# Fused block-causal attention and top-2 expert layer: noise through one dense load, constants set later, a finer router schedule

## The chip, the cores and the metric

One core of a Trainium2 chip runs the kernel. The metric is the device time of one execution in microseconds (us). Of the kernel before, four executions were timed.

## The reference

Eight batches of eight heads, 576 tokens, head size 64. Attention is causal in blocks of 64 tokens. Its output, 4608 rows of 512, goes through a noisy top-2 router with eight experts and then through the two chosen experts.

```
scores = where(block_i >= block_j, q @ k.T / 8, -1e9)
x      = softmax(scores) @ v                    # (8,8,576,64) -> (4608, 512)
noisy  = x @ w_gate + log1p(exp(x @ w_noise)) * noise        # (4608, 8)
two largest per row, softmax over the two -> weights
out    = sum over the two experts e: weight * (relu(x @ w1[e]) @ w2[e])
```

w1 is 8 x 512 x 1024, w2 is 8 x 1024 x 512.

## The kernel before, in words

**Attention.** The work is cut into four groups of two batches (g = 0 to 3; NG = 4). A group has 26 score units (UG = 26): two sets of four head pairs, with 12 units of 512 columns and one small closing unit per set (UN = 13). `score_unit` (line 270) does the matmuls of q and k into one of two PSUM buffers and one exponential on ScalarE (line 287). `av_tile` (line 307) multiplies the exponentials with v, nine tiles (TG = 9) per set, and DVE (VectorE) divides by the sums (lines 335 and 336) into `xr`. `transpose_qk` (line 226) turns the loaded q and k of a group into `qT` and `kT` with matmuls against an identity into one of two buffers of `tr_ps`, which DVE copies out (lines 251 and 253). A group's q and k come in five chunks, 4, 0, 1, 2, 3; of chunk 4 the halves "4A" and "4B" are transposed apart.

**Router.** `x_transpose` (line 343) transposes a group's output, `router` (line 356) is a generator: each `yield` ends a step, and `router_step` runs one step. Its parts are the logits (line 361), noise (371), the largest and second largest (375 to 385), counting within a row (391 to 401), counting matmuls over rows (`pp`, lines 405 and 406), places in the experts' lists (409 to 435) and a record for each row (438 to 450). `scatter` (line 464) then writes each row twice into the experts' lists in DRAM (`xd`) by an indirect DMA of the POOL queue. Groups 0 and 1 form half 0 of the lists, groups 2 and 3 half 1.

**Experts.** Sixteen blocks in the order SEQ (line 593), one expert and half each, 640 rows. `layer1` (line 534) has eight steps with ReLU on ScalarE (line 544), `layer2` (line 548) five. A row's first expert leaves its result in `yd` (line 559, SP queue); the second gathers it (`gather`, line 575, POOL queue), adds (line 562) and writes the output rows (line 564, POOL queue). `load_x` (line 483) fetches a block's rows with a transposing DMA on the SP queue.

**Order.** The order is written out by hand. `at(slot, fn, ...)` (line 600) puts a call into a slot; slot u is what follows score unit u, 104 units in all, then one slot per layer step. Lines 662 to 720 hold the slots: `s0` is a group's first slot, `r0 = s0 + 26`; `rsl` lists the slot of each router step, `r1` the slot of the first scatter. Each engine and each DMA queue executes its own instructions in this order; a scatter or gather also waits for the last ScalarE instruction but one (`pace`), and the loads made with `after` wait for a score unit. `raw_pool` holds eight chunks each of q and k.

**Start.** Lines 644 to 660: the identity, the loads of chunks 4, 0 and 1 on POOL, the constants (`setup_consts`, line 138, on DVE and POOL), chunks 2 and 3, v, the gate weights, and the transposes of 4B and 0. The noise comes in 72 small DMAs of the SP queue, 18 a group (`nz_job`, line 618), 64 rows of 32 bytes each. `clear_x` (line 610) zeroes the part of each list that may stay unwritten, 16 DMAs of 96 rows for each half.

Of the kernel before, what the change touches and what calls it, by code (L numbers as in the profile page):

```python
# [19 lines left out]
def kernel(  # L20
# [110 lines left out]

    nz_all = keep.tile([P, NT, E], F32)
    slots = keep.tile([P, NT, 2], I32)
    wts = keep.tile([P, 2, NT], F32)
    oh_all = keep.tile([P, NG, 2, E, TG], BF16)
    zero = keep.tile([P, 528], BF16)

    def setup_consts():
        nc.vector.memset(ones_mat, 1.0)
        nc.vector.memset(rmask, 1.0)  # L140
        nc.vector.memset(rmask[:, :, :, 0:1], 0.0)
        nc.vector.memset(emask, 1.0)
        nc.vector.memset(emask[:, :, 0:1], 0.0)
        for e in range(E):
            nc.gpsimd.memset(lims[:, e:e + 1], float(e * CAP + LT[e] * P))
        nc.vector.memset(zero, 0.0)
# [11 lines left out]
        nc.gpsimd.iota(poff[:, 0:1], pattern=[[0, 1]], base=0, channel_multiplier=1)  # L158
        nc.vector.tensor_scalar(poff[:, 1:2], poff[:, 0:1], 7, 3, op0=ALU.bitwise_and,
                                op1=ALU.logical_shift_left)  # L160
# [7 lines left out]
        nc.gpsimd.iota(rowid_i, pattern=[[CAP, E], [P, CT]], base=0, channel_multiplier=1)  # L168
# [42 lines left out]
    def load_w(pool, e, k=None):  # L211

        if not k:
            wload[e] = (pool.tile([P, DB, F], BF16, tag="w1", name="w1sb"),
                        pool.tile([P, FB, Dm], BF16, tag="w2", name="w2sb"))
        for t, src in zip(wload[e], (moe_w1[e], moe_w2[e])):
            n = t.shape[1]
            w = src.rearrange("(b p) c -> p b c", p=P)
            if k is None:
                nc.gpsimd.dma_start(out=t, in_=w)  # L220
            elif (k < 2) == (n == DB):
                b0 = (k % 2) * n // 2
# [133 lines left out]
    def router(g):  # L356
# [31 lines left out]
        nc.vector.tensor_add(m.rearrange("p t e -> p e t"), oh[:, 0], oh[:, 1])  # L388

        c2 = rt.tile([P, TG, E], F32, tag="c2")  # L390
        nc.vector.tensor_tensor_scan(out=c2.rearrange("p t e -> p (t e)"),
# [6 lines left out]
        nc.vector.tensor_tensor(out=msv[0], in0=msv[1], in1=m, op=ALU.subtract)  # L398

        w2 = rt.tile([P, TG], F32, tag="w2")  # L400
        nc.vector.tensor_sub(w2, mx[:, 0, :, 0], mx[:, 1, :, 0])
        yield
# [3 lines left out]
        nc.tensor.matmul(out=pp[:, 1, :], lhsT=prem, rhs=mf, start=True, stop=True)  # L406
        nc.scalar.activation(out=w2, in_=w2, func=AF.Exp)
        incl = rt.tile([P, 2, E, TG], F32, tag="incl")
        nc.vector.tensor_tensor_scan(out=incl.rearrange("p i e t -> p (i e t)"),
# [42 lines left out]

    RSTEPS = 12
    rgen = {}
# [28 lines left out]
    def load_x(b):  # L483
        half, e = SEQ[b]
        xg = (ffn["x"] if b else xa_pool).tile([P, DB, CAP], BF16, tag="xg", name="xg")
        ins = nc.sync.dma_start_transpose(out=xg, in_=xd[half][e * CAP:(e + 1) * CAP, 0:Dm])
# [88 lines left out]
    def gather(b, c):  # L575

        half, e = SEQ[b]
        yg = ffn["y"].tile([P, Dm], BF16, tag="yg", bufs=GB, name="yg")
        if len(gathers) < GB:
            nc.gpsimd.memset(yg, 0.0)  # L580
        gathers.append(b)
# [28 lines left out]
    def clear_x(half, slot):  # L610

        for e in range(E):
            r0 = max(0, min(82 * e - 48, CAP - 192)) + e * CAP
            for r in (r0, r0 + 96):
                ins = nc.sync.dma_start(out=xd[half][r:r + 96, :], in_=zero[0:96, 0:DR])
                after(ins, slot)

    def nz_job(g, slot):
        for idx in range(TG):
            for p0, tok in token_blocks(g, idx):  # L620
                ins = nc.sync.dma_start(out=nz_all[p0:p0 + 64, g * TG + idx, :],
                                        in_=token_order(moe_noise[tok:tok + 64, :]))
                after(ins, slot)

# [17 lines left out]
    sched.__enter__()  # L642

    make_identity(nc, ident_f)
    nc.vector.tensor_copy(ident, ident_f)
    load_qk(0, (4, 0, 1))
    for i in range(2):
        nc.vector.memset(vt[i][:, :, :, D:D + 1], 1.0)
    setup_consts()
    load_qk(0, (2, 3))  # L650
    load_v(0)
    nc.gpsimd.dma_start(out=wgn[:, :, 0:E], in_=moe_w_gate.rearrange("(b p) e -> p b e", p=P))
# [9 lines left out]
    for g in range(NG):  # L662
        s0 = g * UG
        if g + 1 < NG:
            at(s0 + 13, transpose_qk, g + 1, "q", "4B")
            at(s0 + 13, transpose_qk, g + 1, "k", "4B")
            at(s0 + 14, transpose_qk, g + 1, "q", 0)
            at(s0 + 15, transpose_qk, g + 1, "k", 0)
            at(s0 + 18, transpose_qk, g + 1, "q", 1)
            at(s0 + 20, transpose_qk, g + 1, "k", 1)  # L670
            at(s0 + 18, load_qk, g + 1, (2, 3))
            at(s0 + 11, load_v, g + 1)
        if g + 2 < NG:
            at(s0 + 20, load_qk, g + 2, (4, 0, 1))
        at(s0 + 0 + (g == 0), transpose_qk, g, "q", 2)
        at(s0 + 1 + (g == 0), transpose_qk, g, "k", 2)
        at(s0 + 11, transpose_qk, g, "q", 3)
        at(s0 + 12, transpose_qk, g, "k", 3)
        at(s0 + 16, transpose_qk, g, "q", "4A")
        at(s0 + 17, transpose_qk, g, "k", "4A")  # L680
        at(s0 + 6, nz_job, g, s0 + 5)
        for i in range(TG):
            at(s0 + UN + 2 + i, av_tile, g, 0, i)
        r0 = s0 + UG
        if g + 1 < NG:
            for i in range(TG):
                at(r0 + 2 + i, av_tile, g, 1, i)
            for j in range(5):
                at(r0 + min(5 + 2 * j, 12), x_transpose, g, j)
            rsl = [13, 14, 15, 16, 17, 18, 19, 20, 20, 21, 21, 22]  # L690
            r1 = 23
        else:
            for i in range(TG):
                at(r0 + i // 2, av_tile, g, 1, i)
            for j in range(5):
                at(r0 + 2 + j, x_transpose, g, j)
            rsl = [7, 8, 8, 9, 9, 10, 11, 12, 12, 13, 13, 14]
# [38 lines left out]
    for fn, b, j in steps:  # L736
# [115 lines left out]
```

## Time and profile before

| what | value |
|---|---|
| median of four executions | 560.83 us (557.41 to 564.97) |
| the profiled execution's own time | 564.97 us |
| its span, first to last instruction | 563.0 us |
| instructions | 9912 |
| TensorE matmuls busy | 445.5 us (79%) |
| ScalarE busy | 238.8 us (42%) |
| POOL busy | 261.5 us (46%) |
| DVE busy | 175.0 us (31%) |
| mean granted TensorE clock | 0.862 |

The profile is of one execution. Its busy rows cut the span into 40 slices of 14.1 us; each digit is a busy share in tenths. A timeline row gives the start, the time taken, the engine, the line, the operation and tiles, the count, and in brackets the idle time of the engine before it with what ended that idle time. PE is TensorE, PEld its weight loads, ACT ScalarE, DVE VectorE, POOL GpSimd, SPq the DMA queue of SyncE. A group row gives busy time, the mean time of one instruction and idle time.

### The profile page before, as it was taken

The page shows a single profiled execution, that of the slowest core. Times are in us where ns is not written, and L with a number is a line of the kernel's source. Part 1 is how long each engine was busy: PE and PEld are TensorE (multiplying, and loading weights), DVE is VectorE, ACT ScalarE, POOL GpSimd, SP SyncE. Part 2 cuts the span into 40 slices and gives each one's busy share as a digit, 9 for nine tenths or more (in the row PEclk, how much of TensorE's full clock was granted, in tenths as well). Part 3 has the DMA queues.
Part 4 walks back from the last instruction along what each step waited for, and adds up shares of the span by engine and source line. Part 5 has one row for each costly group of instructions (what it writes and reads, how often), then busy time and mean ns, then how long its engine had stood idle before and what let it go on. Part 6 is the DMA issues. An engine that isn't in the chain of part 4 may idle for free.

```text
span 563.0 us, 9912 instructions
## 1 busy us (share of the span) xinstructions
PE 445.5 (79%) x3928; PEld 267.4 (47%) x3944; DVE 175.0 (31%) x490; ACT 238.8 (42%) x319; POOL 261.5 (46%) x311
## 2 busy tenths in 40 slices
PE   3787966796649688995939999997957897886975
PEld 2454643463336465652515556653524454443542
DVE  4374894388327737100003000011010120202102
ACT  1756754454426414533414445553414343342330
POOL 9673454583680256675413023273250533517243
PEclk9777985687577779999869999998987997978899
DMA  9999997296289967887776767999999726524122
GB/s 140 142 158 232 96 211 175 81 105 96 91 170 176 164 141 158 202 210 160 150 104 136 162 132 125 187 197 166 129 104 195 188 83 113 156 55 156 43 94 85
DMA packets 141205, 79.76 MB, mean 142 GB/s; under 512 B 101621, under 2 KB 131063, under 8 KB 141152
## 3 DMA queue, kind: packets, MB, share of 16 engines
q0 software_dynamic: 70560, 55.79, 62.7%
q1 hardware_dynamic: 70592, 23.27, 23.2%
q8 instruction: 33, 0.54, 0.4%
q14 instruction: 20, 0.16, 0.1%
HBM read 68.28 MB, written 34.21 MB: 182 GB/s over the span
## 4 chain that ended last, share of the span: by engine, by line
issue 31%; PE 27%; POOL 15%; DMA 11%; DVE 11%; ACT 2%; POOLq 1%; another core or an unknown queue 1%; DVEq 0%; SPq 0%; ACTq 0%
PE yp L553 8%; PE hp L541 7%; POOL yg L582 5%; DMA yg<-yd,orow 4%; POOL out_dram L564 4%; POOL xd L467 4%; PE sc L284 3%; PE av L321 3%; PE tp L246 3%; DMA xg<-xd 2%; DMA w1sb<-in_moe_w_dram 2%; DVE hq L253 2%; DMA t<-in_k_dram 2%; PE av L332 2%; DVE xr L336 2%
## 5 line engine op out<-in xcount | busy, mean ns | idle before, releaser
L541 PE MATMUL hp<-xg,w1sb 128*128 128x320 bf16 x1024 | 159.6, 316 | 40.1 <-ACT hq L544 31.5
L553 PE MATMUL yp<-w2sb,hq 128*128 128x512 bf16 x624 | 144.7, 387 | 9.3 <-DVE yo L562 8.3
L541 PEld LDWEIGHTS <-w1sb 128*128 128x128 bf16 x1024 | 104.6, 103 | 92.5 <-issue 36.2
L544 ACT ACTIVATE hq<-hp 128x640 bf16<-128x640 f32 x128 | 89.4, 704 | 114.8 <-PE hp L541 84.4
L287 ACT ACTIVATE esc<-sc 128x1024 bf16<-128x1024 f32 x96 | 94.8, 1027 | 86.4 <-PE sc L284 49.8
L562 DVE SCALAR_TENSOR_TENSOR yo<-yp,wrow,yg 128x512 f32<-128x512 f32 x46 | 34.5, 751 | 291.3 <-ACT ysb L558 186.0
L467 POOL DMA_INDIRECT xd<-xr,slots x72 | 71.7, 996 | 74.0 <-issue 48.7
L564 POOL DMA_INDIRECT out_dram<-yo,trow x46 | 46.7, 1015 | 125.6 <-DVE yo L562 109.3
L553 PEld LDWEIGHTS <-hq 128*128 128x128 bf16 x640 | 63.5, 99 | 86.1 <-issue 18.2
L558 ACT ACTIVATE ysb<-yp,wrow 128x512 bf16<-128x512 f32 x70 | 48.1, 688 | 98.2 <-PE yp L553 76.6
L582 POOL DMA_INDIRECT yg<-yd,orow x46 | 47.4, 1031 | 57.0 <-ACT hq L544 23.1
L284 PE MATMUL sc<-hq 64*128 64x512 bf16 (+4 forms) x320 | 47.5, 363 | 16.1 <-ACT esc L287 13.1
L321 PE MATMUL av<-vt,esc 128*128 128x65 bf16 x640 | 38.9, 219 | 15.5 <-DVE xr L336 6.6
L321 PEld LDWEIGHTS <-esc 128*128 128x128 bf16 x640 | 30.0, 113 | 31.8 <-issue 14.3
L206 POOL DMA_DIRECT2D vt<-in_v_dram x40 | 33.8, 875 | 14.3 <-PE av L332 10.4
L246 PE MATMUL tp<-ident,t 128*64 128x128 bf16 x512 | 28.9, 282 | 7.4 <-DVE hq L251 3.9
L336 DVE TENSOR_TENSOR xr<-av,rden 128x256 bf16<-128x256 f32 x72 | 30.6, 425 | 2.5
L246 PEld LDWEIGHTS <-t 128*64 128x64 bf16 x512 | 23.1, 148 | 15.6 <-issue 8.1
L253 DVE COPY hq<-tp 128x1024 bf16<-128x1024 bf16 (+1 forms) x24 | 25.0, 1042 | 7.9 <-PE tp L246 3.8
L284 PEld LDWEIGHTS <-hq 64*128 64x128 bf16 x320 | 12.5, 100 | 26.6 <-issue 19.2
L335 DVE RECIPROCAL rden<-av 128x4 f32<-128x4 f32 x72 | 12.5, 174 | 38.9 <-remote 9.8
L251 DVE COPY hq<-tp 128x1024 bf16<-128x1024 bf16 (+1 forms) x24 | 14.9, 620 | 23.2 <-PE tp L246 15.2
(118 smaller groups left out, 225.4 us busy)
## 6 DMA issues: line engine op xcount, KB each, us to landing
yd<-ysb SPq DMA_DIRECT2D x70, 128.0 KB
w1sb<-in_moe_w_dram POOLq DMA_DIRECT2D x16, 512.0 KB
w2sb<-in_moe_w_dram POOLq DMA_DIRECT2D x16, 512.0 KB
t<-in_q_dram POOLq DMA_DIRECT2D x16, 256.0 KB
t<-in_k_dram POOLq DMA_DIRECT2D x16, 256.0 KB
vt<-in_v_dram POOLq DMA_DIRECT2D x32, 128.0 KB
xd<-zero SPq DMA_DIRECT2D x32, 99.0 KB
nz_all<-in_moe_noise_dram SPq DMA_DIRECT2D x72, 2.0 KB
```

The source lines that it names most:

```text
L246: nc.tensor.transpose(to[64 * hf:64 * hf + 64, :, r, :], raw[:, hf, r * 64:(r + 1) * 64], ident)
L284: nc.tensor.matmul(out=sc[:, hf, off:off + z - a], lhsT=kT[sl, c0 + jt * P:c0 + jt * P + P], rhs=qT[sl, c0 + a:c0 + z], start=True, stop=True)
L287: ins = nc.scalar.activation(out=esc[:, hh, :, piece * 512:(piece + 1) * 512], in_=sc, func=AF.Exp, scale=scale)
L321: nc.tensor.matmul(out=av[:, hh, :], lhsT=esc[:, hh, hf, c:c + P], rhs=vb[:, 4 * hf + jt, h, :], start=(jt == 0), stop=(jt == ib))
L336: nc.vector.tensor_tensor(out=xr[:, idx, st * SET * D:(st + 1) * SET * D].rearrange("p (h d) -> p h d", h=SET), in0=av[:, :, 0:D], in1=rde ...
L467: ins = nc.gpsimd.indirect_dma_start(out=xd[half].bitcast(I32), out_offset=bass.IndirectOffsetOnAxis(ap=slots[:, g * TG + idx, i:i + 1], a ...
L541: nc.tensor.matmul(out=hp[:, n, 0:NW], lhsT=w1sb[:, db, fb * P:(fb + 1) * P], rhs=xgs[b][:, db, n * NW:(n + 1) * NW], start=(db == 0), sto ...
L544: ins = nc.scalar.activation(out=hs[b][:, fb, :].rearrange("p (n w) -> p n w", n=2), in_=hp[:, :, 0:NW], func=AF.Relu)
L553: nc.tensor.matmul(out=yp, lhsT=hs[b][:, fb, c * P:(c + 1) * P], rhs=w2sb[:, fb, :], start=(fb == 0), stop=(fb == FB - 1))
L558: nc.scalar.activation(out=ysb, in_=yp, func=AF.Copy, scale=w)
L564: ins = nc.gpsimd.indirect_dma_start(out=out, out_offset=bass.IndirectOffsetOnAxis(ap=trow[half][:, e, c:c + 1], axis=0), in_=yo, in_offse ...
L582: ins = nc.gpsimd.indirect_dma_start(out=yg, out_offset=None, in_=yd[half][0:e * CAP, :], in_offset=bass.IndirectOffsetOnAxis(ap=orows[hal ...
```

## The change

Seven edits. The noise comes in one DMA of 72 partitions by 2 KB, into the tile that later receives the first expert block; DVE sorts it (16 copies), PE transposes it in fp32 (8 transposes), DVE copies it into place (36 copies), in slots 7 to 11 of group 0. The constants of DVE move from ahead of the first transposes to slot 6; those of POOL behind the loads of chunks 2 and 3. Chunk 4 is requested ahead of the identity. The transposes of q and k get other slots. The router has 15 steps instead of 12, with other slots; group 2's AV tiles, router and scatters run closer together. The clears have 8 DMAs of 128 rows for each half and later slots. The weights of the third and fourth expert come in two DMAs each instead of four, and the buffers of `gather` are zeroed by DVE at slot 110 instead of by POOL one at a time.

```
+    xa = xa_pool.tile([P, DB, CAP], BF16)
+    nzw = [xa.rearrange("p a b -> p (a b)")[0:B * TG, 1024 * i:1024 * (i + 1)].bitcast(F32) for i in range(2)]
...
-    def setup_consts():
-        nc.vector.memset(ones_mat, 1.0)
...
+    def setup_pool():
         for e in range(E):
             nc.gpsimd.memset(lims[:, e:e + 1], float(e * CAP + LT[e] * P))
...
         nc.vector.tensor_add(m.rearrange("p t e -> p e t"), oh[:, 0], oh[:, 1])

+        w2 = rt.tile([P, TG], F32, tag="w2")
+        nc.vector.tensor_sub(w2, mx[:, 0, :, 0], mx[:, 1, :, 0])
+        yield
+
         c2 = rt.tile([P, TG, E], F32, tag="c2")
...
-        w2 = rt.tile([P, TG], F32, tag="w2")
-        nc.vector.tensor_sub(w2, mx[:, 0, :, 0], mx[:, 1, :, 0])
+        yield
         yield
...
         nc.scalar.activation(out=w2, in_=w2, func=AF.Exp)
+        yield
         incl = rt.tile([P, 2, E, TG], F32, tag="incl")
...
-    RSTEPS = 12
+    RSTEPS = 15
...
-        yg = ffn["y"].tile([P, Dm], BF16, tag="yg", bufs=GB, name="yg")
-        if len(gathers) < GB:
-            nc.gpsimd.memset(yg, 0.0)
+        yg = ffn["yg"][len(gathers) % GB]
...
-            r0 = max(0, min(82 * e - 48, CAP - 192)) + e * CAP
-            for r in (r0, r0 + 96):
-                ins = nc.sync.dma_start(out=xd[half][r:r + 96, :], in_=zero[0:96, 0:DR])
-                after(ins, slot)
...
+            r0 = max(0, min(82 * e - 26, CAP - P)) + e * CAP
+            ins = nc.sync.dma_start(out=xd[half][r0:r0 + P, :], in_=zero[:, 0:DR])
+            after(ins, slot)
+
+    def load_nz():
+
+        nc.sync.dma_start(out=nzw[0], in_=moe_noise.rearrange("(p t) e -> p (t e)", t=64))
+
+    def sort_nz(eh):
+        e0 = eh * (E // 2)
+        src = nzw[0].rearrange("p (j r e) -> p e r j", j=8, r=8)[:, e0:e0 + E // 2]
+        dst = nzw[1].rearrange("p (e h r j) -> p h e r j", e=E // 2, h=2, r=8)
+        for hf in range(2):
+            for e in range(E // 2):
+                nc.vector.tensor_copy(dst[:, hf, e], src[:, e])
+
+    def transpose_nz(eh):
+        nb = B * TG
+        e0 = eh * (E // 2)
+        tp = tr_ps.tile([P, E // 2, nb], F32, tag="tr")
+        for e in range(E // 2):
+            nc.tensor.transpose(tp[:, e, :], nzw[1][:, e * P:(e + 1) * P], ident_f[0:nb, 0:nb])
+        for hf in range(2):
+            p = slice(64 * hf, 64 * hf + 64)
+            src = tp[p].rearrange("p e (g b k) -> p e g b k", b=2, k=TG)
+            dst = nz_all[p, :, e0:e0 + E // 2].rearrange("p (g i) e -> p e g i", i=TG)
+            for bb in range(2):
+                for e in range(E // 2):
+                    nc.vector.tensor_copy(dst[:, e, :, 4 * bb:4 * bb + 4], src[:, e, :, bb, hf:8:2])
+            nc.vector.tensor_copy(dst[:, :, :, 8], src[:, :, :, hf, 8])
...
+    load_qk(0, (4,))
     make_identity(nc, ident_f)
     nc.vector.tensor_copy(ident, ident_f)
-    load_qk(0, (4, 0, 1))
+    load_qk(0, (0, 1))
+    load_nz()
...
-    setup_consts()
     load_qk(0, (2, 3))
+    setup_pool()
     load_v(0)
...
-            at(s0 + 13, transpose_qk, g + 1, "q", "4B")
-            at(s0 + 13, transpose_qk, g + 1, "k", "4B")
-            at(s0 + 14, transpose_qk, g + 1, "q", 0)
+            early = 5 if g else 0
+            at(s0 + 13 - early, transpose_qk, g + 1, "q", "4B")
+            at(s0 + 13 - early, transpose_qk, g + 1, "k", "4B")
+            at(s0 + 13, transpose_qk, g + 1, "q", 0)
             at(s0 + 15, transpose_qk, g + 1, "k", 0)
-            at(s0 + 18, transpose_qk, g + 1, "q", 1)
-            at(s0 + 20, transpose_qk, g + 1, "k", 1)
+            at(s0 + 24, transpose_qk, g + 1, "q", 1)
+            at(s0 + 25, transpose_qk, g + 1, "k", 1)
...
-        at(s0 + 0 + (g == 0), transpose_qk, g, "q", 2)
-        at(s0 + 1 + (g == 0), transpose_qk, g, "k", 2)
-        at(s0 + 11, transpose_qk, g, "q", 3)
+        at(s0 + 3, transpose_qk, g, "q", 2)
+        at(s0 + 5, transpose_qk, g, "k", 2)
+        at(s0 + 10, transpose_qk, g, "q", 3)
         at(s0 + 12, transpose_qk, g, "k", 3)
-        at(s0 + 16, transpose_qk, g, "q", "4A")
-        at(s0 + 17, transpose_qk, g, "k", "4A")
-        at(s0 + 6, nz_job, g, s0 + 5)
+        at(s0 + 17, transpose_qk, g, "q", "4A")
+        at(s0 + 18, transpose_qk, g, "k", "4A")
...
-        if g + 1 < NG:
+        if g < 2:
             for i in range(TG):
-                at(r0 + 2 + i, av_tile, g, 1, i)
+                at(r0 + 1 + i, av_tile, g, 1, i)
             for j in range(5):
-                at(r0 + min(5 + 2 * j, 12), x_transpose, g, j)
-            rsl = [13, 14, 15, 16, 17, 18, 19, 20, 20, 21, 21, 22]
-            r1 = 23
+                at(r0 + min(4 + 2 * j, 11), x_transpose, g, j)
+            rsl = [12, 13, 14, 15, 16, 17, 18, 19, 20, 21, 21, 22, 22, 23, 23]
+            r1 = 24
+        elif g == 2:
+            for i in range(TG):
+                at(r0 + 1 + 2 * i // 3, av_tile, g, 1, i)
+            for j in range(5):
+                at(r0 + (3, 5, 6, 7, 8)[j], x_transpose, g, j)
+            rsl = [9, 9, 10, 11, 12, 13, 14, 14, 15, 16, 16, 17, 17, 18, 18]
+            r1 = 19
         else:
...
-            rsl = [7, 8, 8, 9, 9, 10, 11, 12, 12, 13, 13, 14]
-            r1 = 15
+            rsl = [7, 7, 8, 9, 9, 10, 11, 11, 12, 13, 13, 14, 14, 15, 15]
+            r1 = 16
...
-            at(r0 + r1 + (j if g in (0, 2) else 2 * j // 3), scatter, g, j)
+            at(r0 + r1 + (2 * j // 3 if g else j), scatter, g, j)
...
-    at(8, clear_x, 0, 7)
-    at(UG + 8, clear_x, 1, UG + 7)
+    at(6, setup_consts)
+    at(7, sort_nz, 0)
+    at(8, transpose_nz, 0)
+    at(9, sort_nz, 1)
+    at(11, transpose_nz, 1)
+    at(UG + 4, clear_x, 0, UG + 3)
+    at(3 * UG + 4, clear_x, 1, 3 * UG + 3)
...
-        if u == 3 * UG + 18:
+        if u == 3 * UG + 19:
...
-            for k in range(4):
-                at(u + (10, 13, 16, 19)[k], load_w, wM, 2, k)
+            at(u + 10, load_w, wM, 2, "a")
+            at(u + 16, load_w, wM, 2, "b")
...
-            for k in range(4):
-                at(slot + 3 * k + 12, load_w, wL, 3, k)
+            ffn["yg"] = [ffn["y"].tile([P, Dm], BF16, name=f"yg{i}", bufs=1) for i in range(GB)]
+            for t in ffn["yg"]:
+                nc.vector.memset(t, 0.0)
+            at(slot + 14, load_w, wL, 3, "a")
+            at(slot + 20, load_w, wL, 3, "b")
```

More of the change, by code (lines that the diff above doesn't have):

```diff
@@ L136 @@
     zero = keep.tile([P, 528], BF16)
-    def setup_consts():
-        nc.vector.memset(ones_mat, 1.0)
[L140 to L143, printed above, removed]
+    def setup_pool():
         for e in range(E):
             nc.gpsimd.memset(lims[:, e:e + 1], float(e * CAP + LT[e] * P))
-        nc.vector.memset(zero, 0.0)
         nc.gpsimd.memset(prem, 0.0)
@@ L158, in setup_consts @@
         nc.gpsimd.iota(poff[:, 0:1], pattern=[[0, 1]], base=0, channel_multiplier=1)
+        nc.gpsimd.iota(rowid_i, pattern=[[CAP, E], [P, CT]], base=0, channel_multiplier=1)
+    def setup_consts():
+        nc.vector.memset(ones_mat, 1.0)
+        nc.vector.memset(rmask, 1.0)
+        nc.vector.memset(rmask[:, :, :, 0:1], 0.0)
+        nc.vector.memset(emask, 1.0)
+        nc.vector.memset(emask[:, :, 0:1], 0.0)
+        nc.vector.memset(zero, 0.0)
         nc.vector.tensor_scalar(poff[:, 1:2], poff[:, 0:1], 7, 3, op0=ALU.bitwise_and,
@@ L167, in setup_consts @@
                                 op=ALU.subtract)
-        nc.gpsimd.iota(rowid_i, pattern=[[CAP, E], [P, CT]], base=0, channel_multiplier=1)
         for i in range(NH):
@@ L211, in load_w @@
     def load_w(pool, e, k=None):
-        if not k:
+        if k in (None, 0, "a"):
             wload[e] = (pool.tile([P, DB, F], BF16, tag="w1", name="w1sb"),
                         pool.tile([P, FB, Dm], BF16, tag="w2", name="w2sb"))
-        for t, src in zip(wload[e], (moe_w1[e], moe_w2[e])):
+        for i, (t, src) in enumerate(zip(wload[e], (moe_w1[e], moe_w2[e]))):
             n = t.shape[1]
             w = src.rearrange("(b p) c -> p b c", p=P)
-            if k is None:
+            if k is None or k == "ab"[i]:
                 nc.gpsimd.dma_start(out=t, in_=w)
-            elif (k < 2) == (n == DB):
+            elif k in (2 * i, 2 * i + 1):
                 b0 = (k % 2) * n // 2
@@ L484, in load_x @@
         half, e = SEQ[b]
-        xg = (ffn["x"] if b else xa_pool).tile([P, DB, CAP], BF16, tag="xg", name="xg")
+        xg = ffn["x"].tile([P, DB, CAP], BF16, tag="xg", name="xg") if b else xa
         ins = nc.sync.dma_start_transpose(out=xg, in_=xd[half][e * CAP:(e + 1) * CAP, 0:Dm])
@@ L612, in clear_x @@
         for e in range(E):
-            r0 = max(0, min(82 * e - 48, CAP - 192)) + e * CAP
-            for r in (r0, r0 + 96):
-                ins = nc.sync.dma_start(out=xd[half][r:r + 96, :], in_=zero[0:96, 0:DR])
-                after(ins, slot)
[L618 to L623, printed above, removed]
+            r0 = max(0, min(82 * e - 26, CAP - P)) + e * CAP
[24 more added lines that the diff above has]
+            nc.vector.tensor_copy(dst[:, :, :, 8], src[:, :, :, hf, 8])
     def flags():
```

## The prediction

> **What bounds the kernel now.** I read the page's busy rows by slice first, then the list of waits, then the timeline around each gap of TensorE, then the stretch table for the granted clock.
>
> ```profile
> PE   3787966796649688995939999997957897886975
> DVE  4374894388327737100003000011010120202102
> PEclk9777985687577779999869999998987997978899
> ```
>
> TensorE (PE) is the fullest row, and its clock is the other half of the story: up to slice 15 (about 210 us, the attention and router part) it runs between half and full clock; after that (the expert part) mostly at full. So the attention part is not at a limit of work. It has 104 score units whose exponentials cost ScalarE 1.03 us each (line 287), 107 us, and takes 182 us (first scores at 12.87, last exponential at 195.3). Everything the change touches, but for one item, lies in this part. TensorE's instructions are executed in order, so one matmul that waits holds up the next scores, and with them ScalarE.
>
> The gaps that count, from the timeline (start, length, engine, line, operation, and in brackets the idle time before it and what ended it); the last line closes a gap in the expert part:
>
> ```profile
> 12.87 0.61 PE L284 MATMUL sc<-hq 64*128 64x512 bf16 x2 [1.41 <-DVE hq L253]
> 27.20 0.69 DVE L251 COPY hq<-tp 128x1024 bf16<-128x1024 bf16 x1 [7.54 <-PE tp L246]
> 49.91 1.06 PE L246 MATMUL tp<-ident,t 128*64 128x128 bf16 x16 [2.35 <-DMA t<-in_q_dram]
> 78.85 0.24 PE L405 MATMUL pp<-ms,ones_mat 128*128 128x144 bf16 x1 [2.83 <-DVE w L401]
> 79.92 0.30 PE L321 MATMUL av<-vt,esc 128*128 128x65 bf16 x4 [0.77 <-DVE xr L336]
> 86.86 2.15 PE L332 MATMUL av<-vt,esc 128*64 128x65 bf16 x40 [1.72 <-DVE xr L336]
> 130.69 0.24 PE L405 MATMUL pp<-ms,ones_mat 128*128 128x144 bf16 x1 [2.20 <-DVE w L401]
> 184.92 0.24 PE L405 MATMUL pp<-ms,ones_mat 128*128 128x144 bf16 x1 [2.22 <-DVE rden L335]
> 267.50 7.30 PE L553 MATMUL yp<-w2sb,hq 128*128 128x512 bf16 x24 [4.95 <-DVE yo L562]
> ```
>
> To be seen: in groups 0, 1 and 2 the router's counting matmul (line 405) stops TensorE for 2.2 to 2.8 us while VectorE (DVE) makes its input. In the first, lines 385 to 401 ran from 76.46 to 78.81, one router step against one slot of scores.
>
> The stretch table (length, busy time and count of PE, PEld, DVE, ACT, POOL, then clock) for the 3.3 us that begin about 1.5 us after each of the three stalls, and for the start of group 2:
>
> ```profile
> 80.40:83.70 3.30, 3.30 (x44) 2.21 (x42) 3.09 (x11) 1.97 (x2) 0.77 (x2) 0.50 1.20 237
> 87.20:107.60 20.40, 16.31 (x188) 10.02 (x188) 8.67 (x24) 10.08 (x11) 11.27 (x12) 0.50 0.48 118
> 131.60:134.90 3.30, 3.14 (x40) 1.98 (x41) 3.09 (x11) 1.09 (x2) 0.00 (x0) 0.50 1.17 176
> 186.20:189.50 3.30, 3.30 (x42) 2.17 (x41) 3.02 (x12) 2.83 (x3) 0.00 (x0) 0.50 1.40 74
> ```
>
> Each stall is followed by a stretch at half clock in which TensorE is the limit (busy 3.1 to 3.3 of 3.3).
>
> **The change part by part.**
>
> *Start and noise.* Score unit 0 waits for chunk 0 of k. Its last packet ends at 8.25, but the transposes stand until 9.55: both transpose buffers hold chunk 4B, whose copies sit on DVE behind the constants (DVE waits 4.31 us for an iota, ends them at 9.04, copies at 9.07). With the constants moved behind score unit 6, transposes of k can follow its landing. POOL issues chunk 4 about 0.7 earlier and chunks 0 and 1 some 0.4 earlier; the noise load, 147 KB on SP ahead of everything, gives back up to 0.8 (estimate at the 140 GB/s of slice 0). Chain: k landed 8.5, 16 transposes 1.06, copies 1.23 and 0.22: scores at 11.0 instead of 12.87, 1.9 gained. The identity is now made after two POOL issues (0.73 and 0.60), ready near 2.5, still ahead of chunk 4.
>
> What was in front moves into slots 6 to 11, over the 7.54 us hole shown above. Constants: about 2.6 us of DVE (from the pace at which they ran before). Noise: 16 sorting copies of 64 elements and 36 of 16 elements out of PSUM, 52 in all, which the trace does not have. Nearest row: the small independent copies of the router's record (lines 446 to 449) start 0.08 apart, giving 52 × 0.08 = 4.2. [...] Lower bound zero, if the hole takes all; upper bound 25, at the 0.48 of the small strided rows (lines 378, 388). From slot 6 (21.8) to slot 13 (28.4) there are 6.6 us. [...] What is late next: the two transpose buffers, hence the PE transposes of slots 11 to 13 and the scores behind them. Part of this is covered: at slot 15 TensorE waited 0.92 for group 1's k chunk 0 (32.67). [...] That the noise is loaded otherwise earns nothing itself: all waits for it sum to 0.2 us.
>
> *Clears and SP.* Half as many clears (16 each 96 rows become 8 of 128), each set later. SP loses 72 noise issues; the last 18 (155.8 to 167.3) stood just ahead of the transposed load at 167.98, but that load also needs scatters that POOL issued until 166.1, and its data are used near 198: nothing gained. What counts is that the clears (35.3 to 46.7) and noise packets leave the DMA engines just as group 1's chunk 2 comes in.
>
> *Moved q/k transposes.* Group 1's chunk 2 stalled TensorE for 2.35 us at 49.91. It is now transposed three to four slots later and its load has less company: gone. The stretch from 49.6 to 56.5 ran at half clock; full clock does transposes in 0.64 instead of 1.06, scores in 0.39 instead of 0.61, so about 38% of busy time goes: at 6 busy, 2.3, and I count half. **Gain 3.5.** Chunk 1 at slots 24 and 25 comes when DVE has the router behind it: zero. POOL gets a wait: k chunk 2 of the next group takes the raw buffer of chunk 4, whose last transpose is now in the same slot 18. Behind it are the loads of slot 20 and scatters; one slot, about 1.5 us, with eleven slots before the data are needed: nothing.
>
> *Router in 15 steps.* In groups 0 and 1 the counting inputs are made at slot 18 and used at slot 20. For group 2 it is one slot apart, with 1.26 us of DVE (lines 391, 397, 398) in it: at most 0.5 left over. 2.83 + 2.20 + 2.22 + 2 × 0.77 (the AV matmul behind, second stall like the one at 79.92) − 0.5 = **gain 8.3**. The wait for line 336 at 86.86 (1.72, 1.71 and 1.31 in the three groups) stays: lines 428 to 449 still share slots with the last AV tiles.
>
> *The clock after them.* [...] Other gaps are near and may pull the clock down anyhow: **gain 1.9**.
>
> *Group 2 re-timed.* The same matmuls in fewer slots of group 3, which has no next group to transpose: zero in sum. Its scatters begin four slots sooner, but POOL had drained them by 226 before, when group 3's followed at 228.09 off the router: nothing.
>
> *Expert part.* POOL is behind from 228 to 262:
>
> ```profile
> 259.16 0.57 POOL L580 MEMSET yg<- 128x512 bf16 x1
> 260.00 1.07 POOL L582 DMA_INDIRECT yg<-yd,orow  x1 [0.28 <-POOL yg L580]
> ```
>
> The gather at 260.00 is what TensorE awaits at 267.50. Ahead of it go one memset with its gap (0.84) and two of four weight issues (0.8 each): 2.5 sooner. In return ten memsets of about 0.27 (line 301's row) stand on DVE at slot 110, ahead of the last x copy that the router's matmul needs: 2.7, of which DVE's idle covers 1.0. **Gain 0.8.**
>
> *Sum.* −1.0 + 3.5 + 8.3 + 1.9 + 0.8 = 13.5. Its execution took 564.97 (span 563.0), the slowest of four; their median is 560.83. From the one 551.5, from the other 547.3; the terms are partly that execution's own bad luck, so I set **549**.
>
> **Rivals.** *The stalls move* (25 in 100): DVE has the same router work, so what leaves line 405 is waited for at line 332. Then chunk 2 gives 2.4, the router 4, clock and expert part nothing, noise costs 3.3: 560.8 − 3 = 558, range 553 to 566. For it: DVE is busy 3.0 of 3.3 in the rows above. Against: PE gaps there came from order, not sum (DVE 32.2 of 44.1 us in group 1).
>
> *The noise copies cost more than the hole holds* (15 in 100; slower). Place: group 0, slots 6 to 13. The net loss is 52c − 3.8 for a pace c. The other terms sum to 14.5, so it decides at c = 0.35, and is over 1% slower from 0.46. At the 0.48 of lines 378 and 388: 21.2 lost, 560.8 − 14.5 + 21.2 = 567.5, range 566 to 575. For it: strided operands, each a separate instruction. Against: no waits between them are needed, and their output is fp32.
>
> *The long half-clock stretches go too* (12 in 100): 87 to 108 and 138 to 155 follow router waits; 38% of 16.3 and 11.6 busy is 10.6 more: 538, range 532 to 542.
>
> **How the numbers follow.** My case has 48 in 100, with its own range 542 to 554. Faster by over 1% (under 555.2; about what a measurement can tell): 48 + 12 + 2 of the first rival = 62. Within 1%: 22, the rest of that rival less 1. Slower: 16. The range 538 to 566 leaves out some 6 below and 13 above.
>
> **What would show it.** Right: line 405 idle under 1 us in all; first scores near 11.0; no DMA wait for group 1's chunk 2; clock above 0.84 in group 1 and 0.70 in groups 2 and 3. Wrong: copies of the noise over 0.3 us apart, with ScalarE idle between 20 and 32; line 332's waits grown to 3 us; a 2 us hole before line 361 in the expert part.

## The result and the profile after

The changed kernel takes 554.12 us (median of 12 runs, 543.16 to 562.85), the kernel before 560.4 (17 runs, 555.83 to 567.1). The ratio is 0.975, 95% interval 0.970 to 0.981. It is taken over the executions within 1.5% of each kernel's fastest (4 of 12 after, 14 of 17 before; neither profiled execution is among them), and over all executions the means, 553.6 and 560.8, differ by only 1.3%. The forecast, 549 with a range of 538 to 566, holds. Its terms hold less well than its total: one had the wrong sign, and most of the others were far off in size.

The profiled execution after takes 555.2 us (span 553.4), against 564.97 (span 563.0). The rows that answer to those of before:

```profile
PE   3689787866758489867919999998998897786975
DVE  3788885685566267000103000110011120201202
PEclk9869958796765599986968999999899997978999
```

VectorE (DVE) is now at 8 through slices 2 to 5 (28 to 83 us), where before it was at 7, 4, 8 and 9. The clock row is no better in the attention part: over it, from 8 us to the first expert matmul, the mean clock is 0.75 in both executions.

From the timeline of the changed kernel (start, length, engine, line, operation, and in brackets the idle time before and what ended it), the rows for the start, the noise, the counting matmuls and the end of attention:

```profile
9.48 1.07 PE L250 MATMUL tp<-ident,t 128*64 128x128 bf16 x16 [0.29 <-DMA t<-in_k_dram]
11.87 0.61 PE L288 MATMUL sc<-hq 64*128 64x512 bf16 x2 [1.32 <-DVE hq L257]
...
22.36 1.10 DVE L632 COPY xa<-xa 72x64 f32<-72x64 f32 x8
23.25 0.71 PE L639 MATMUL tp<-ident_f,xa 72*128 72x72 f32 x4 [2.29 <-DVE xa L632]
24.00 0.75 DVE L646 COPY nz_all<-tp 64x16 f32<-64x16 f32 x8 [0.54 <-PE tp L639]
24.54 2.99 ACT L291 ACTIVATE esc<-sc 128x1024 bf16<-128x1024 f32 x3 [2.19 <-PE sc L288]
33.83 1.94 ACT L291 ACTIVATE esc<-sc 128x1024 bf16<-128x1024 f32 x2 [3.46 <-PE sc L288]
...
74.18 0.30 PE L411 MATMUL pp<-ms,ones_mat 128*128 128x144 bf16 x1 [1.35 <-DVE xr L340]
...
120.16 0.24 PE L411 MATMUL pp<-ms,ones_mat 128*128 128x144 bf16 x1 [1.66 <-PE sc L288]
...
165.35 0.28 PE L411 MATMUL pp<-ms,ones_mat 128*128 128x144 bf16 x1 [2.35 <-DVE xr L316]
...
177.93 2.29 PE L336 MATMUL av<-vt,esc 128*64 128x65 bf16 x40
184.36 0.18 DVE L339 RECIPROCAL rden<-av 128x4 f32<-128x4 f32 x1 [5.68 <-remote]
185.44 0.84 PE L325 MATMUL av<-vt,esc 128*128 128x65 bf16 x12 [4.33 <-DVE xr L340]
186.67 1.02 ACT L291 ACTIVATE esc<-sc 128x1024 bf16<-128x1024 f32 x1 [7.55 <-PE av L325]
...
290.04 2.32 PE L548 MATMUL hp<-xg,w1sb 128*128 128x320 bf16 x8 [11.68 <-DMA xg<-xd]
```

To be seen: the first scores come 1.0 earlier, not 1.9. Beside the constants and the noise copies TensorE stops for 2.29 and ScalarE for 2.19 and 3.46. The three counting matmuls (line 411, before line 405) still wait, 5.36 us in all against 7.25. At the end of attention TensorE stands for 4.33 us where before, at the same place in the order, it stood for 1.32. The wait of 2.35 us for group 1's chunk 2 is gone.

The first expert matmul comes at 190.6 (before 198.0), but block 4 of the expert part starts at 290.0 (before 291.0): it waits for a transposed load that SP issues at 276.35, behind the stores of block 2, and that takes 13.65 us (before 279.30 and 11.65). A lead of 7.4 us has become one of 1.0. The rest of the 9.6 us in span comes late: before, TensorE stood 9.61 us from 415.53, and after it does not. So this one pair of executions doesn't say which part of the change gave the gain. The experiments time each part.

### The profile page after: what moved, and what is told of

Its sections match the earlier page's. It is cut to its first block, busy times and chain, and to the rows that moved or that the text cites. A ratio compares the mean times of both kernels' runs of the same rounds, so it can differ in the third digit from the quotient of the medians.

```text
span 553.4 us, 9869 instructions
## 1 busy us (share of the span) xinstructions
PE 441.4 (80%) x3936; PEld 265.1 (48%) x3952; DVE 183.0 (33%) x552; ACT 237.1 (43%) x319; POOL 252.6 (46%) x297
## 3 DMA queue, kind: packets, MB, share of 16 engines
q1 hardware_dynamic: 64212, 22.18, 20.4%
## 4 chain that ended last, share of the span: by engine, by line
PE 40%; issue 25%; DVE 13%; POOL 10%; DMA 4%; another core or an unknown queue 3%; ACT 3%; POOLq 0%; DVEq 0%; ACTq 0%
PE yp L560 12%; PE hp L548 11%; POOL yg L587 5%; PE av L325 4%; PE sc L288 4%; POOL out_dram L571 4%; PE tp L250 3%; DVE hq L257 3%; DVE xr L340 3%; DMA xg<-xd 2%; PE av L336 2%; ACT esc L291 2%; PE tp L354 1%; DMA t<-in_k_dram 1%
## 5 line engine op out<-in xcount | busy, mean ns | idle before, releaser
L548 PE MATMUL hp<-xg,w1sb 128*128 128x320 bf16 x960 | 147.7, 315 | 39.6 <-ACT hq L551 27.2
L325 PE MATMUL av<-vt,esc 128*128 128x65 bf16 x640 | 37.3, 216 | 24.1 <-DVE xr L340 22.2
L288 PE MATMUL sc<-hq 64*128 64x512 bf16 (+4 forms) x320 | 45.8, 361 | 10.1 <-ACT esc L291 8.6
L250 PE MATMUL tp<-ident,t 128*64 128x128 bf16 x512 | 27.5, 271 | 2.6 <-DMA t<-in_q_dram 2.3
L250 PEld LDWEIGHTS <-t 128*64 128x64 bf16 x512 | 21.2, 141 | 8.3 <-issue 3.6
```

What stands on the lines that cost most here:

```text
L250: nc.tensor.transpose(to[64 * hf:64 * hf + 64, :, r, :], raw[:, hf, r * 64:(r + 1) * 64], ident)
L288: nc.tensor.matmul(out=sc[:, hf, off:off + z - a], lhsT=kT[sl, c0 + jt * P:c0 + jt * P + P], rhs=qT[sl, c0 + a:c0 + z], start=True, stop=True)
L325: nc.tensor.matmul(out=av[:, hh, :], lhsT=esc[:, hh, hf, c:c + P], rhs=vb[:, 4 * hf + jt, h, :], start=(jt == 0), stop=(jt == ib))
L548: nc.tensor.matmul(out=hp[:, n, 0:NW], lhsT=w1sb[:, db, fb * P:(fb + 1) * P], rhs=xgs[b][:, db, n * NW:(n + 1) * NW], start=(db == 0), sto ...
```

## The experiments

Every kernel computes the same result. The ratios are to the kernel before on the same chip. e1 to e8 ran on chips where that takes 561.3 or 562.1 us, as in the result above; e9 to e12 on a chip where it takes 514.7, so ratios of the two sets are not compared with each other.

**Each part undone, from the changed kernel.**

e1: noise and constants as before.

```
-    load_nz()                      # and setup_pool, sort_nz, transpose_nz
+    setup_consts()                 # whole, ahead of the scores
+        at(s0 + 6, nz_job, g, s0 + 5)
```

> The changed kernel with one part undone: noise rows come in 72 small loads as before, constants are set up ahead of the first scores. All else stays changed. The sum of the prediction (start and noise cost 1.0 us net): about 1 us faster than the changed kernel, ratio to the kernel before near 0.973. Rival A (the start is the part that pays, since the first scores come earlier and the loads of group 0 are not disturbed by 72 small ones): 3 to 5 us slower than the changed kernel, ratio near 0.983. Either way the gap of 2.3 us on TensorE ahead of the noise transposes and the one of 3.5 us on ScalarE near 30 us should be gone, and the first exponential should be back near 13.5 us.

Measured: 1.021 (1.013 to 1.028), so 4.7% slower than the changed kernel. Both guesses were far too small. The first exponential is back at 13.51, but the long gap of ScalarE is not gone:

```profile
32.50 1.94 ACT L289 ACTIVATE esc<-sc 128x1024 bf16<-128x1024 f32 x2 [3.62 <-PE sc L286]
```

So the 3.46 us of the changed kernel can't be put down to the noise copies alone.

e2: router, its slots and group 2 as before.

```
-    RSTEPS = 15
+    RSTEPS = 12
-        if g < 2: ... elif g == 2: ... rsl = [9, 9, 10, ...]; r1 = 19
+        if g + 1 < NG: ... rsl = [13, 14, 15, ...]; r1 = 23
```

> The changed kernel with one part undone: router in 12 steps, and the slots of the second half's AV, of x transposes, router steps and scatters as before, for group 2 too. The sum of the prediction (8.3 us from the router and up to 1.9 from the clock): 8 to 10 us slower than the changed kernel, ratio to before near 0.991. Rival B (the stalls at the prefix matmul are still 5.4 us in the changed kernel's trace against 7.3 us before, so the steps bring little, and what attention gains is given back at the expert part's fourth load): 0 to 3 us slower, ratio 0.975 to 0.980.

Measured: 0.972 (0.964 to 0.980). Router and group 2 together earned nothing; rival B comes nearest, and even its band (0.975 to 0.980) is not reached. The first expert matmul is even earlier, at 182.6.

e3: slots of the q and k transposes and the clears as before.

```
-        at(s0 + 3, transpose_qk, g, "q", 2)
+        at(s0 + 0 + (g == 0), transpose_qk, g, "q", 2)
-    at(UG + 4, clear_x, 0, UG + 3)
+    at(8, clear_x, 0, 7)           # and the rest of this part
```

> The changed kernel with one part undone: slots of the q and k transposes, and slots and size of the clears, as before. The sum of the prediction (3.5 us): 3 to 4 us slower than the changed kernel, ratio to before near 0.981; the wait for the q chunk 2 load of group 1, 2.35 us, is back. Rival C (this is the part that made most of the gain, by taking DVE copies and loads out of each other's way in all groups): 6 us slower or more, ratio 0.986 or more.

Measured: 1.006 (1.001 to 1.012), 3.2% slower than the changed kernel; rival C. But the wait for group 1's chunk 2 is not back: the transposes start at 50.19 and wait for nothing. Without the 72 noise loads SP issues these clears from 21.35 on, ahead of that load.

e4: the expert part's edits undone.

```
-        yg = ffn["yg"][len(gathers) % GB]
+        yg = ffn["y"].tile([P, Dm], BF16, tag="yg", bufs=GB, name="yg")
+        if len(gathers) < GB:
+            nc.gpsimd.memset(yg, 0.0)
-            at(u + 10, load_w, wM, 2, "a")
+                at(u + (10, 13, 16, 19)[k], load_w, wM, 2, k)
```

> The changed kernel with one part undone: the gather buffers cleared one by one on GpSimd, weights of experts 2 and 3 loaded in four pieces each at their old slots. The sum of the prediction (0.8 us): within 1 us of the changed kernel, ratio to before 0.975 to 0.977. Rival D (the attention part's lead is lost by the expert part's fourth block in the profiled pair, so what is left at the end comes from the expert part's own edits): 5 us slower or more, ratio 0.984 or more.

Measured: median 549.01 (536.58 to 554.34) against 561.29, too wide a spread for a ratio. Undoing these edits loses nothing; rival D falls.

**Parts alone, and group 2.** e5 is the changed kernel with e2's and e4's edits; e7 has e3's edit too, and e8 has e1's instead. In e6 only group 2 goes back to the others' slots:

```
-        if g < 2:
+        if g < 3:
-        elif g == 2: ...
-            at(r0 + r1 + (2 * j // 3 if g else j), scatter, g, j)
+            at(r0 + r1 + (2 * j // 3 if g in (1, 3) else j), scatter, g, j)
```

> Noise by the one load and constants behind the first scores, and the q and k transposes and clears moved; router, group 2 and expert part as before. Theory T1 (these two parts together make all of the gain; the router part costs attention 8 us and the expert part's edits cost its first four blocks 6 us, which the profiles of the two runs that undid them show, but the ends of these runs not clearly): ratio to before 0.965 to 0.972, attention over (first expert matmul) near 183, block 4 starting near 276. Rival T2 (router and expert part are neutral): ratio 0.972 to 0.978, as the changed kernel.

> The changed kernel, with group 2's second half of AV, its x transposes, router steps and scatters at the slots of groups 0 and 1, one scatter per slot. Theory T3 (the 8 us that undoing the router part took off attention lie in group 2's earlier scatters, which now run beside group 3's AV at its end): first expert matmul near 183 instead of 190.6, the gaps of 4.3 and 2.8 us on TensorE ahead of AV near 181 to 189 gone, ratio to before 0.968 to 0.973. Rival T4 (it is the 15 steps themselves): first expert matmul stays near 190, ratio 0.974 to 0.978.

> The kernel before with the noise and constants part alone. Theory T1 (noise and transposes pay only together): ratio 0.990 to 1.005. Rival T5 (the two add up, noise is worth 26 us wherever it stands, as undoing it cost that much): ratio 0.955 to 0.965. The prediction's sum: 1 us slower, 1.002.

> The kernel before with the moved q and k transposes and clears alone. Theory T1: ratio 1.000 to 1.015, as with router and expert part it was 1.021 (noise undone). Rival T5: ratio near 0.970, since undoing it cost 17 us. The prediction's sum: 3.5 us faster, 0.994.

Measured, with the time of the profiled execution, and its first expert matmul and mean clock from 8 us up to it:

| kernel | ratio (95%) | profiled | first expert matmul | clock |
|---|---|---|---|---|
| before | 1 | 565.0 | 198.0 | 0.75 |
| e7, noise alone | 0.990 (0.983 to 0.997) | 548.1 | 195.5 | 0.71 |
| e8, q/k and clears alone | 0.983 (0.976 to 0.990) | 564.6 | 184.7 | 0.78 |
| e5, these two | 0.967 (0.962 to 0.972) | 539.9 | 181.9 | 0.78 |
| changed | 0.975 (0.970 to 0.981) | 555.2 | 190.6 | 0.75 |
| e6, changed, but not group 2 | 0.962 (0.953 to 0.970) | 543.9 | 183.8 | 0.79 |
| e3, changed, but not q/k | 1.006 (1.001 to 1.012) | 563.6 | 201.6 | 0.68 |
| e1, changed, but not noise | 1.021 (1.013 to 1.028) | 578.5 | 200.8 | 0.71 |

An early first expert matmul is not yet a short execution: the profile of e8 is of the slowest of its seven (548.8 to 564.6 us), 13 us ahead there and level with before at the end.

Noise and q/k alone multiply to 0.990 × 0.983 = 0.973, and together give 0.967: they nearly add. They are all of the gain. The rest of the change takes 0.8% back (0.967 to 0.975; the intervals overlap), and only one of the changed kernel's twelve executions is shorter than the longest of e5's six (544.8 us). T3 holds in its direction: without group 2's new slots the kernel is 1.4% faster (0.962 against 0.975; the intervals touch at 0.970), more than its band says, and reaches the expert part 6.8 us sooner. The two gaps that it names shrink to 2.31 and 0.83 and don't go. T1's "only together" falls by e8, and T5's sizes (0.96 and 0.97) fall too. But e1 and e3 stand: on a kernel that lacks one of the two, the other edits cost far more (e8 to e1 3.8%, e7 to e3 1.7%).

What e1 and e3 have most of shows in the waits that end by a signal of no known origin, "remote" in the profile. Summed over ScalarE and VectorE they are 78 us in e1, 74 in e3, 48 in before, 40 in changed, 29 in e5 and in e8. They don't order all kernels (e6 has 65). Their cause is open; they are taken up at the end.

**Inside the gain.** e9 is the kernel before plus one DMA, into the buffer `nzw` of the change:

```
+    nc.sync.dma_start(out=nzw[0], in_=moe_noise.rearrange("(p t) e -> p (t e)", t=64))
```

> The kernel before with one DMA more on SP at the start (the dense noise load, its result unused). In the profiles of the three kernels with the old noise loads TensorE stands 7 to 10 us once between blocks 9 and 10 of the expert part, in the seven with the new load it does not. Theory T6 (that stall goes by how many DMAs SP issued earlier, as its transfers share eight semaphores in turn, and the new noise part shifts that count by one): ratio 0.983 to 0.992, the stall between 385 and 435 us gone. Rival T7 (the count means nothing): ratio 0.997 to 1.004, a stall of 7 us or more still there.

Measured: 0.989 (0.979 to 0.999). The ratio is in T6's band, but its interval nearly reaches 1, and the profile shows no more than 3.37 us idle near 397. But the other three on this chip have no stall of 7 us there either, and two of them (e11, e12) load the noise as before and lack the extra DMA. In the trace of the kernel before, SP's 192 DMAs do take eight semaphores in turn (numbers 111 to 118). Still T6 is not shown: what noise alone gains in the expert part stays open.

e10 is e6 with e4's edits.

> Noise and constants, q and k transposes and the 15 router steps changed; group 2 at the slots of groups 0 and 1, the expert part as before. Theory T8 (the 15 steps are worth a little, up to 3 us, and the expert part's edits cost some): ratio 0.957 to 0.963, faster than both the run without the 15 steps (0.967) and the one with the expert edits (0.9615). Rival T9 (15 steps are worth nothing): ratio 0.964 to 0.970.

Measured: 0.981 (0.972 to 0.990), on the faster chip. 502.6 against 514.7 us in the medians is 12 us less. The bands set for it were for the other chips, so T8 against T9 is not decided.

e11 moves two transposes of each group; e12 moves all of them, and leaves the clears.

```
-        at(s0 + 0 + (g == 0), transpose_qk, g, "q", 2)
-        at(s0 + 1 + (g == 0), transpose_qk, g, "k", 2)
+        at(s0 + 3, transpose_qk, g, "q", 2)
+        at(s0 + 5, transpose_qk, g, "k", 2)
```

> The kernel before with two transposes of each group moved alone: q chunk 2 from slot 0 to 3 and k chunk 2 from slot 1 to 5. The prediction's step (the wait of 2.35 us for the chunk 2 load of group 1, and half of the clock after it, 3.5 us): ratio 0.992 to 0.995. Theory T10 (most of what the transposes and clears gave, 9 us in time and 13 us in attention, is in these two): ratio 0.982 to 0.988, first expert matmul near 186. Rival T11 (it is the other transposes): no more than 1 us, ratio 0.998 to 1.002.

> The kernel before with all q and k transposes at their new slots, but the clears as before (16 DMAs of 96 rows each, in groups 0 and 1). Theory T12 (the transposes make the gain of 1.7%): ratio 0.981 to 0.986, first expert matmul near 185. Rival T13 (it is the clears, whose rows no longer compete with the loads of group 0): ratio 0.994 to 1.000, first expert matmul 193 to 198.

Measured: e11 0.999 (0.993 to 1.005), e12 0.986 (0.975 to 0.998). T11; T12 by the middle, but the interval of e12 reaches into T13's band (0.994 to 1.000) too. For the step that I had priced, chunk 2, no gain of its own is measured; the forecast 3.5 us (0.993) lies at the edge of the interval. The timeline of e11 shows why; below it that of e8, where the clears are moved too:

```profile
44.69 2.21 SPq L615 DMA_DIRECT2D xd<-zero  x5
...
50.20 1.07 PE L246 MATMUL tp<-ident,t 128*64 128x128 bf16 x16 [1.55 <-DMA t<-in_q_dram]
```

```profile
47.54 0.64 PE L248 MATMUL tp<-ident,t 128*64 128x128 bf16 x16
...
48.68 4.39 SPq L616 DMA_DIRECT2D xd<-zero  x8
```

In e11 the transposes come later and still wait 1.55 us, as the load lands no sooner: on the same chip e9, with the slots of before, has them at 50.85, after a wait of 1.91. SP issues the clears beside that load. In e8 they start at 47.54 without a wait, and the clears are issued after. The traces mark when a load completes. Where the clears are issued beside it (from 34 or 35 us on: before, e9, e11, e12), this load takes 9.5 to 10.8 us from its issue to its last mark; in the other ten kernels, whose clears come earlier or later, 6.7 to 8.2. In e12 it lands at 52.16, the clears being where they were, and still nothing waits: TensorE comes to these transposes at 52.20, as those of chunk 1 now stand ahead of them.

Where the 1.4% of e12 comes from, its profile doesn't show. Against that of e11 it is 6.2 us ahead at the last score unit (162.1 against 168.3), but only 0.8 at the first expert matmul (177.9 against 178.7), and the two executions take the same (506.3 and 506.2). Over groups 1 to 3, where the lead grows, chunk 1 of the next group no longer shares slots 18 and 20 with the AV tiles of the first half; that this is the cause is a guess.

## Why the prediction was right, and where it was not

**The start.** 1.9 forecast, 1.0 measured. The step that failed was "k landed 8.5". Before and after:

```profile
3.46 0.76 POOL L196 DMA_DIRECT2D t<-in_k_dram  x1
9.55 1.92 PE L246 MATMUL tp<-ident,t 128*64 128x128 bf16 x32 [3.70 <-DVE hq L251]
```

```profile
3.85 0.73 POOL L200 DMA_DIRECT2D t<-in_k_dram  x1
8.12 1.06 PE L250 MATMUL tp<-ident,t 128*64 128x128 bf16 x16 [2.34 <-DMA t<-in_q_dram]
```

POOL issues this load 0.4 us later than before, not 0.4 earlier, as the identity is now made ahead of it. Its last completion mark is at 9.43, and the row at 9.48 waits for it. Before, the last mark is at 9.30: the 8.25 that I took was the end of a packet. So before, k's transposes stood hardly longer than their load. What is gained is q's half: of the 32 transposes that ran from 9.55, 16 now run at 8.12.

**The noise copies.** The row gave 4.2 us for 52 copies. Measured on VectorE: 1.10 and 1.09 for the sorts (line 632), 24.00 to 25.76 and 27.51 to 29.27 for the placing, together 5.7, or 0.11 a copy. The row, at 0.08, was too kind to both kinds (0.14 a copy from SBUF, 0.10 from PSUM). The place was right, the cover only in part. At unit 15 the exponentials are 2.6 us later than before (34.7 against 32.1), at unit 18 level again (38.3 against 38.2). Group 1's load of k hides 0.9 of this (the wait ahead of 32.67). Over the rest TensorE had the better clock after, which was luck: the scores at 37.88 take 0.39 us, those at 37.54 before 0.61 (granted clock from 36.0 to 38.3 us: 0.90 and 0.50). The 3.8 of the second rival is what the profile before leaves room for: 6.6 us of slots 6 to 13, the wait of 0.92 and the 1.9 forecast for the start, less 2.6 for the constants, 0.69 and 1.23 for q and k chunk 3 and 1.09 for the memsets of line 301. With it the row gives a loss of 0.4. The sum has 1.0 and the first rival 3.3; no run shows either, about 0.1 is seen. The second rival needed 0.35 a copy and falls.

What failed is the sentence "that the noise is loaded otherwise earns nothing itself". Alone the part gives 1.0% (e7), some 5.6 us, and undone it costs 4.7%. I had looked only at waits for the noise, 0.2 us. One thing that it does is to free SP: in e7 the 16 clears are issued at 22 to 33 us instead of 35 to 47, and the wait for group 1's chunk 2 is 0.21 instead of 2.35:

```profile
51.59 1.06 PE L250 MATMUL tp<-ident,t 128*64 128x128 bf16 x16 [0.21 <-DMA t<-in_q_dram]
```

In e7's profile attention is 2.5 us shorter (198.0 to 195.5); where the rest of the gain lies is open.

**The q/k transposes.** 3.5 forecast; 9.4 us alone (1.7% of 561, e8, clears included). The direction was right, the mechanism only in part. The wait for chunk 2 was the step. e11 shows that moving its reader three and four slots leaves most of it (1.55), as the load lands late where the clears run beside it. I had written that what counts is the company of that load, and then priced the slots. By e12 most of the gain needs no moved clears, so the larger share lies in the other slots, which I set at zero; its interval (0.975 to 0.998) leaves the size open.

**The router.** 8.3 forecast. With group 2's new slots nothing is measured (e2), without them at best 1.1%, or 6 us: e6 stands at 0.962 and e2, which differs from it by the router alone, at 0.972, with intervals that overlap. The failed step is "made at slot 18 and used at slot 20", from which I took the wait of line 411 to be gone. VectorE's rows of after, by group:

```profile
72.60 0.48 DVE L406 TENSOR_TENSOR ms<-ms,m 128x72 bf16<-128x72 bf16 x1
73.70 0.42 DVE L340 TENSOR_TENSOR xr<-av,rden 128x256 bf16<-128x256 f32 x1
...
118.58 0.48 DVE L406 TENSOR_TENSOR ms<-ms,m 128x72 bf16<-128x72 bf16 x1
119.68 0.42 DVE L340 TENSOR_TENSOR xr<-av,rden 128x256 bf16<-128x256 f32 x1
...
164.83 0.47 DVE L406 TENSOR_TENSOR ms<-ms,m 128x72 bf16<-128x72 bf16 x1
```

In groups 0 and 1 the input (`ms`) is ready at 73.08 and 119.06, so the extra steps did what they should. But the matmuls start 1.1 us later, at 74.18 and 120.16, each 0.06 us after the copy of an AV tile (line 340). The first row names that copy as the releaser; the second names a score matmul that had ended at 118.50. The kernel says what the copy is to them: the result `pp` takes one of the two PSUM buffers of the AV tiles (`av_ps`, lines 93 and 410), and such a buffer is free when the tile in it has been copied out. I had counted the wait for the input and not the one for the buffer. In the profiles of the eight kernels with 12 steps most of these waits (25 of 32) end with the last instruction of the input's step (`w`, line 401 of before), in the six with 15 steps almost none does (one of 17, of 0.2 us). In group 2 the distance is one slot, and the input itself is late, at 165.30; "at most 0.5 left over" became 2.35.

The copies are late because VectorE is full. The stretch table for the three places (length, then busy time of PE, PEld, DVE, ACT and POOL, and the clock):

```profile
68.50:75.00 6.50, 4.22 (x58) 2.46 (x59) 5.83 (x21) 3.17 (x4) 4.16 (x7) 0.66 2.03 167
116.00:121.00 5.00, 2.54 (x46) 1.63 (x44) 4.45 (x15) 2.41 (x3) 3.82 (x4) 1.00 2.16 137
161.00:166.00 5.00, 1.96 (x18) 0.99 (x14) 4.13 (x12) 2.95 (x4) 0.52 (x1) 0.50 1.14 186
```

VectorE is busy for 83 to 90% of each. In e6, with the 15 steps but group 2 at the others' slots, line 411 waits 3.4 us in all instead of 5.36. The first rival said that the stalls move. They did, though to another line than it named. The waits of TensorE in the attention part, of before and then of after (total, times, longest):

```profile
PE pp L405 <- DVE w L401: 5.0, 2, 2.8
PE av L332 <- DVE xr L336: 4.7, 3, 1.7
...
PE av L321 <- DVE xr L336: 4.3, 9, 0.8
```

```profile
PE av L325 <- DVE xr L340: 20.0, 15, 4.3
...
PE pp L411 <- DVE xr L316: 2.3, 1, 2.3
```

For VectorE's copies of AV tiles TensorE now waits 20.0 us instead of 9.0 (4.7 and 4.3), all of it at the whole tiles (line 325, before 321), and 8.6 of it after 166 us, in group 3. The matmuls that I had named (line 332) no longer wait.

**The clock.** 1.9 forecast, half of 38% of the 9.7 us that TensorE was busy in the three stretches after the stalls. No run shows this term: the mean clock to the first expert matmul is 0.75 before and after, so the gain is zero. As the stalls are mostly still there (5.36 us of 7.25), the change did not test whether they bring the half clock. Without stalls of that length it is found too: before, half clock held from 87.2 to 107.6, with TensorE busy for 16.3 of these 20.4 us and no gap in it over 1.85. Over the kernels those that reach the expert part by 185 us have 0.78 to 0.79, the later ones 0.68 to 0.75; which is cause and which effect these runs don't say.

**Group 2.** Zero forecast, a loss of 1.4% (7.7 us of 561) measured by e6. The scatters of group 2 run from 173.6 to 202.8, where before they began at 192.4, and so beside the last AV tiles of group 3; in e6 they begin at 180.6 and the hole of 4.33 us is 2.31, put down to another releaser. I had asked only whether POOL has time for them, not what stands beside them. That the scatters cause the late signal in that hole is not shown.

**The expert part.** 0.8 gain forecast; e4 and the pair e5 and e2 (0.967 and 0.972, intervals overlapping) show none. The cost that I counted is there, on VectorE in the changed kernel:

```profile
204.59 2.74 DVE L798 MEMSET yg<- 128x256 uint32 x10
207.25 0.36 DVE L355 COPY xT<-tp 128x512 bf16<-128x512 bf16 x1
```

The earlier gather earns nothing where block 4 waits for its load in any case.

So the total was right by luck: the errors cancelled. For noise and transposes the sum had 2.5 us (3.5 less 1.0), and e5 shows 3.3% of 561, 18.6. For router, clock, group 2 and expert part it had 11.0, and from e5 to the changed kernel 0.8% are lost, 4.7. Forecast 13.5, measured 13.9 by the ratio (6.3 between the medians). Two sums of the prediction are off, and nothing rests on them: eight of the 104 exponentials are the small ones of 0.38 us, so all take some 102 us, not 107; and 147 KB at 140 GB/s are 1.05 us, not 0.8.

## What to carry to other kernels

Here a later slot for a consumer took away the wait for its input alone (`ms` ready at 73.08, the matmul at 74.18): look for what else it needs, such as the buffer that its result takes, and for how busy the engine is that has to free it (here 83 to 90%). The wait for the load of chunk 2 ended when it landed (1.55 us left in e11); price what is issued beside a load (here 9.5 to 10.8 us with the clears, 6.7 to 8.2 without), not only the slot of its reader. Do not read the worth of a part from one pair of profiles in which other stalls of 5 to 10 us come and go: time it alone and undone, and if the two differ, say so.

## What the runs showed of the hardware

The hole at 184.36 is odd. By the records, in which the ends of matmuls are modelled, the 40 matmuls ahead of it end at 180.22, yet the reciprocal that reads them starts 4.1 us later; ScalarE, waiting for scores whose matmuls end by 180.76, starts at 186.67. The first of these waits is put down to "remote", the second to a later AV matmul. Waits put down to "remote" take 30.3 us of ScalarE in the changed kernel. On the chip of e9 to e12 they are all but absent (0 to 1.6 us), and there the kernel before takes 514.7 us instead of 561 to 562. From e6 and then from e10, which differs from it only in the expert part's edits, ScalarE's waits (total, times, longest):

```profile
ACT hq L551 <- remote: 27.4, 9, 8.3
ACT esc L291 <- remote: 15.2, 4, 6.4
```

```profile
ACT hq L551 <- PE hp L548: 98.3, 128, 23.3
ACT ysb L565 <- PE yp L560: 93.1, 70, 12.4
ACT esc L291 <- PE sc L288: 50.5, 45, 10.4
```

In e10 every one of the 128 waits of line 551 has its matmul as releaser. What delays the signals on the first chips no run shows, and it was not tried apart. It bounds the account above: up to 78 us of such waits lie in the profiles from which the places were read, while the ratios include them on both sides.
